# Placing the loads of ready weight blocks and of weight conversions in a fused attention, expert and gated-layer kernel

## The chip, the cores and the metric

The kernel runs on one NeuronCore of a Trainium2 chip. The metric is the device time of one execution in microseconds, taken as the median of several runs. The profile is of one execution; all other views come from its trace.

## The reference

The reference is three layers in float32, one after the other. The first is masked attention over four batches of 576 positions and eight heads of 64. The second is a mixture of eight experts over N = 2304 tokens of width 512, in which a Sinkhorn iteration makes the weights P and every token goes through every expert:

```python
for e in range(E):                       # E = 8, w1[e]: 512 x 1024, w2[e]: 1024 x 512
    h = np.maximum(x @ w1[e], 0.0)
    out += P[:, e:e + 1] * (h @ w2[e])
```

The third is a gated layer with 1536 hidden columns:

```python
xn = x / np.sqrt(np.mean(x * x, axis=-1, keepdims=True) + 1e-6) * rms_g
g = xn @ w_gate
silu = g * (1.0 / (1.0 + np.exp(-g)))
return (silu * (xn @ w_val) @ w_out).astype(np.float32)
```

The three weights of the gated layer arrive as float64.

## The kernel before, in words

**Numbers.** Each float32 operand is split into a high and a low part, and a product is made of three matmuls: high by high, high by low, low by high. Large products are cut into two-by-two blocks and done with seven block products in place of eight (`PROD`, L944), so an operand is needed as seven block combinations, each with a high and a low part. A weight region has 14 places of 256 columns: seven high, seven low.

**Stages.** Attention and the first expert come first, up to about 330 us. Then 42 groups `n` follow (L1978), each an expert `g` from 1 to 7, a half of its hidden columns and a third `qd` of the tokens. A group has 14 steps: two regions `j` (rounds r = 0 and 1) of seven products. A step issues one up product (`product`, L1219: six matmuls of 384 columns), its evictions (`outcome_1`, L1358), a tick, one down unit of the group before (`unit`, L1812) and another tick. Group 41 is the last; then come 12 units that are left over (`PRE_UNITS`, L2061), and then the gated layer, in nine passes (L2129): three slices `p` of hidden columns, three token thirds each. A pass has two rounds of 14 steps; step 0 to 6 of a round use one region, step 7 to 13 the next. The pass works with regions 0 to 3 for its slice, so the first round uses regions 0 and 1 and the second round 2 and 3.

**Order of work.** Every engine runs its own program in order. The order is set when the program is written, by a counter `bg.now` that `bg.pump` raises by one: a pump is one *slot*, 28 to a group. `bg.later(1, f)` writes `f` at the next pump. A `Queue` (L81) holds steps with lags in slots: a step is written once its lag has passed since the step before it, at most one slot being made up for a late one. Of the queues, `prep` makes or loads first-layer weights, `prep2` second-layer weights, `norm` the normalised inputs of the gated layer, and `conv` the conversions below. `prep` and `conv` are made with `yields`: once `bg.tight` is set (from expert 7 on, L1981), they write nothing while a model of VectorE's backlog is above a limit; `prep` does so only up to eight items. `drain` writes out what is left under a tag.

**Conversions.** `convert` (L820) turns half a 128-row block of a float64 weight into float32 on VectorE: `load` brings 256 KB into `raw`, `head` (L837, L838), `number` (L844, L848), `tail` (L854, L855) and `whole` (L861) are seven instructions of 256 columns, and `store` writes 128 KB to a table in DRAM (`m2d`). `raw`, the work area `a` and the result `t` are single places in the tile `cv`; `raw` is read last by `tail`, `t` by the store. `conversion` (L869) gives the lags. At group 2 the queue `conv` receives 24 items, then eight combinations (`first_combos`, L885), then 16 items (L2000 to L2006). It stands still in every group whose number divides by three (`conv.paused`, L1999), and at group 39 what is left is written at once (L2011 to L2013). The last 32 items are queued at the second pass (L2142).

`first_combos` loads float32 blocks, makes their seven combinations (L900 is the first instruction, in `sums_1`), splits them and stores them to the table `w1d`: the *ready* weights of the gated layer's first slice, regions 0 to 3.

**Ready weights.** `ready_combos` (L935) loads a part of region 0 or 1 (up to 512 KB, L940) into `w1t`, into places that the last group's products have read. `prepare_1` (L1054) calls it for the parts of `PARTS_AT` after products 1, 3, 5 and 6 of group 41 and puts each into `prep`; `prep.drain(("w1", E, 1))` (L2072) writes out what `prep` still holds after the 12 left units. Right behind it, L2073 to L2079 load regions 2 and 3 in six transfers, 3584 KB in all, into `last_r`, a free x place, and three pieces of `w2t`.

**Normalised inputs.** `norm_blocks` (L1479) makes, per third of the tokens, three times four parts: `plain` and `keep` (stores at L1499), then `add1`, `add2`, four `part` steps (ScalarE and VectorE at L1489 and L1490) and `keep2` (five stores at L1523). The next block's `part` steps write over tiles that `keep2` reads. Their results in `xnd` are loaded as x blocks (`load_block`, L1154), the first ones before the first pass.

All DMAs named here are issued by SyncE (SP), one after the other; an issue waits on SP for what it depends on. The evictions that free the two up-product buffers `ub` are, in the groups, copies on ScalarE and the additions of `with_more` (L1254) on VectorE, and in the passes also the multiplies at L1411 and L1425.

Of the kernel before, what the change touches and what calls it, by code (L numbers as in the profile page):

```python
# [10 lines left out]
U32 = mybir.dt.uint32  # L11
# [103 lines left out]
def kernel(  # L115
# [17 lines left out]
    E, _, F = w1.shape  # L133
# [27 lines left out]
    EARLY = 2  # L161
    EARLY_AT = (5, 6)
    SUMS = 24
    CONV_WAIT = (6, 4)
    PRE_WAIT = 6
    PRE_UNITS = 12
    LAG = 12
    TURN_AT = (29, 30, 31, 32, 33, 34), (32, 33, 34, 35, 36, 37)
# [2 lines left out]
    Y0_AT = (7, 10, 13, 16, 19)  # L171
    READ = 7
    LAST_READ = 16
    STEP = 1.5
    PACE = 1.2
    PARTS_AT = {0: 0, 1: 1, 3: 2, 5: 3, 6: 4}
# [640 lines left out]
        return us  # L817


    def convert(nm, f, half):  # L820

        n = KC * P // 2
        raw = cv[:, : 2 * n].bitcast(U32)
        pair = raw.rearrange("p (n t) -> p n t", t=2)
        a, t = cv[:, 2 * n : 3 * n].bitcast(U32), cv[:, 3 * n : 4 * n]

        def load():
            if nm == "o":
                nc.sync.dma_start(out=raw, in_=m2_out[f * P : (f + 1) * P, half * 2 * n : (half + 1) * 2 * n])
            else:  # L830
                src = (m2_gate if nm == "g" else m2_val)[half * n : (half + 1) * n, f * 2 * P : (f + 1) * 2 * P]
                nc.sync.dma_start(
                    out=raw.rearrange("p (c n) -> p c n", c=KC // 2), in_=src.rearrange("(c p) n -> p c n", p=P)
                )

        def head():
            nc.vector.tensor_scalar(out=a, in0=pair[:, :, 1], scalar1=0x7FFFFFFF, scalar2=None, op0=ALU.bitwise_and)  # L837
            nc.vector.tensor_scalar(  # L838
                out=t, in0=a.bitcast(F32), scalar1=LOW_HEAD, scalar2=HIGH_HEAD, op0=ALU.max, op1=ALU.min
            )  # L840
            return n

        def number():
            nc.vector.tensor_scalar(  # L844
                out=a, in0=t.bitcast(U32), scalar1=3, scalar2=0x3FFFFFFF,
                op0=ALU.logical_shift_left, op1=ALU.bitwise_and,
            )
            nc.vector.scalar_tensor_tensor(  # L848
                out=a, in0=pair[:, :, 1], scalar=0xC0000000, in1=a, op0=ALU.bitwise_and, op1=ALU.bitwise_or
            )  # L850
            return 2 * n

        def tail():
            nc.vector.tensor_scalar(out=t.bitcast(U32), in0=a, scalar1=0xFF800000, scalar2=None, op0=ALU.bitwise_and)  # L854
            nc.vector.scalar_tensor_tensor(  # L855
                out=t, in0=pair[:, :, 0], scalar=2.0**-52, in1=t, op0=ALU.mult, op1=ALU.mult
            )
            return 2 * n

        def whole():  # L860
            nc.vector.tensor_tensor(out=t, in0=a.bitcast(F32), in1=t, op=ALU.add)  # L861
            return n

        def store():
            nc.sync.dma_start(out=m2d[nm][:, f, half * n : (half + 1) * n], in_=t)

        return load, head, number, tail, whole, store

    def conversion(items, wait, quick=False):  # L869

        for n, (nm, f, half) in enumerate(items):
            load, head, number, tail, whole, store = convert(nm, f, half)
            tag = nm, f
            if n == 0:
                conv.add([(WRITE, load)], tag)
            step = 1 if quick else STEP
            conv.add([(wait, head), (step, number), (step, tail)], tag)
            if n + 1 < len(items):
                conv.add([(step, whole), (0 if quick else 1, convert(*items[n + 1])[0])], tag)
                conv.add([(0 if quick else 2, store)], tag)  # L880
            else:
                conv.add([(step, whole), (WRITE, store)], tag)


    def first_combos(s, c):  # L885

# [25 lines left out]
        def high(src):  # L912
            nc.scalar.activation(h[:, : src.shape[1]].bitcast(F32R), src, AF.Copy)
# [7 lines left out]
        def store(src, spots):  # L921
# [4 lines left out]
                        in_=t[:, P * at : P * (at + n)].rearrange("p (k n) -> p k n", k=n),  # L926
                    )

        return load, [
            (PRE_WAIT, sums_1), (STEP, sums_2), (STEP, lambda: high(raw)), (STEP, lambda: low(raw)),  # L930
            (1, lambda: store(raw, ((0, 0, 2), (2, 5, 1), (3, 2, 1)))), (5, lambda: high(both)), (STEP, lambda: low(both)),
            (1, lambda: store(both, ((0, 3, 2), (2, 6, 1)))),
        ]

    def ready_combos(j, part):  # L935

# [117 lines left out]
    def prepare_1(g, j, part=None):  # L1054

        if part is None:
            for part in range(5):
                prepare_1(g, j, part)
            return
        if g == E:  # L1060
            prep.add([(PACE, lambda: ready_combos(j, part))], ("w1", g, j))
        else:
            if part == 0:
                stages[g, j] = combine(region(g, j), raw_1)
            prep.add(stages[g, j][part], ("w1", g, j))
        n = (g, j + 1) if j < 3 else (g + 1, 0)
        if part == 4 and n[0] < E + NPASS and n[0] != E:
            prep.add([(WRITE, lambda: load_1(*n))])
# [463 lines left out]
    with tc.manual_schedule():  # L1532
# [445 lines left out]
        for n, (g, hh, qd) in enumerate(groups):  # L1978
# [20 lines left out]
            conv.paused = n % NQD == 0 and n < NGP - 3  # L1999
            if n == 2:  # L2000
                conversion(conv_items[:24], CONV_WAIT[0])
                for s in range(4):
                    for c in range(2):
                        load, steps = first_combos(s, c)
                        conv.add([(WRITE, load)] + steps, "combos")
                conversion(conv_items[24:40], CONV_WAIT[0])  # L2006
            if ends and n < NGP - 1:
                g2, hh2, _ = groups[n + 1]
# [60 lines left out]
            (w2t[:, 0:3].rearrange("p f s n -> p (f s n)"), (0, 1, 2, 3, 4, 5, 6, 7, 8, 9, 10, 11)),  # L2069
            (xt_flat[:, 7680:8192], (12, 13)),  # L2070
        ])
        prep.drain(("w1", E, 1))  # L2072
        for j, parts in (  # L2073
            (2, ((last_r[:, :1792], 0), (x_slot(gone_x)[:, :1280], 7), (last_r[:, 1792:], 12), (x_slot(gone_x)[:, 1280:], 13))),
            (3, ((w2t[:, 0:3].rearrange("p f s n -> p (f s n)"), 0), (xt_flat[:, 7680:8192], 12))),
        ):
            ready = w1d[:, j].rearrange("p i k c m -> p (i k c m)")
            for t, at in parts:
                nc.sync.dma_start(out=t.bitcast(F32), in_=ready[:, 256 * at : 256 * at + t.shape[1]])  # L2079
        prep.add([(WRITE, lambda: load_1(E + 1, 0))])  # L2080

        def downs(r):
# [46 lines left out]
        for n, (p, qd) in enumerate(passes):  # L2129
# [9 lines left out]
            bg.drain("x")  # L2139
            if n == 1:  # L2140
                conv.yields = False
                conversion(conv_items[40:], CONV_WAIT[1], True)  # L2142
            for j in range(NG // 2):
                gs, hs = {}, {}
                first_round = (n, j) == (0, 0)
# [8 lines left out]
                for ci, s in enumerate((2 * j, 2 * j + 1)):  # L2154
# [8 lines left out]
                    for i, (wk, xk, which, begins) in enumerate(PROD):  # L2163
# [8 lines left out]
                        step = 7 * ci + i  # L2172
                        if first_round:
                            tick()
                            if PRE_UNITS + step < LAG:
                                second(14 * NGP + PRE_UNITS + step)
                            if step in LAST_TURN:
                                t = LAST_TURN.index(step)
                                if t == 0:
                                    spares[NGP - 1] = spare_of(NGP - 1)  # L2180
                                turn_tile(groups[-1][2], t, db[t % 3], spares[NGP - 1])
                        else:
                            bg.pump()
# [54 lines left out]
```

## Time and profile before

| | |
|---|---|
| median of 3 runs | 2094.93 us |
| lowest and highest run | 2087.04 and 2097.82 us |
| profiled execution | 2093.68 us, of which the span of the trace is 2091.9 |
| busy, matmuls on TensorE (PE) | 2009.6 us in 13611 instructions |
| busy, VectorE (DVE) | 1591.9 us |
| busy, ScalarE (ACT) | 1305.5 us |
| busy, GpSimd (POOL) | 268.1 us |
| moved by DMA | 434.24 MB, mean 208 GB/s |

PE is busy nearly throughout, so the engine views that matter are those of its gaps. A wait row names the engine and line that stood, what released it, the total, the count and the longest. A timeline row gives the start, the duration, the instruction and, in brackets, the idle time before it with its releaser; instructions of one kind in a row are merged. SPq is the queue of SP; a merged SPq row spans from the first issue to the end of the last, waits included. The clock is the granted share of 2.4 GHz.

### The profile page before, as it was taken

How to read it: one execution, taken by the hardware profiler on the slowest of the kernel's cores; microseconds unless marked ns; L12 is line 12 of the kernel's file. 1: busy time of each engine (PE TensorE's matmuls, PEld its weight loads, DVE VectorE, ACT ScalarE, POOL GpSimd, SP SyncE). 2: the span in 40 equal slices, each digit the busy share in tenths (PEclk: the TensorE clock that was granted, in tenths of full speed). 3: DMA queues.
4: the chain of work that ended last, by engine and by line, in shares of the span. 5: the costliest groups of instructions: out<-in, count | busy, mean ns of one | idle time of the engine just before them, and what ended most of it. 6: DMA issues, size and time to landing. Idle time of an engine off the chain costs nothing. (4 is left out here: it accounts for less than half of the span.)

```text
span 2091.9 us, 37504 instructions
## 1 busy us (share of the span) xinstructions
PE 2009.6 (96%) x13611; PEld 1920.0 (92%) x13611; DVE 1591.9 (76%) x3387; ACT 1305.5 (62%) x2932; POOL 268.1 (13%) x304
## 2 busy tenths in 40 slices
PE   8999999999999999999999999999998689999999
PEld 7888888999999999999999999999997578888998
DVE  3777747979786887968787798888888677887644
ACT  6766325777776877768787777777765433423332
POOL 6443200010211111111011101110100000000000
PEclk9999999999999999999999999999999999999999
DMA  6687576677988989796888978888666875354341
GB/s 182 174 241 212 171 262 203 216 256 190 270 208 223 245 222 278 194 277 190 240 230 226 260 196 239 216 217 234 157 214 218 270 226 177 118 176 139 112 166 61
DMA packets 356297, 434.24 MB, mean 208 GB/s; under 512 B 81296, under 2 KB 258384, under 8 KB 355984
## 3 DMA queue, kind: packets, MB, share of 16 engines
q1 hardware_dynamic: 317344, 363.48, 53.6%
q0 software_dynamic: 38768, 68.36, 18.6%
q8 instruction: 107, 1.75, 0.3%
q14 instruction: 78, 0.64, 0.1%
HBM read 301.75 MB, written 130.02 MB: 206 GB/s over the span
## 5 line engine op out<-in xcount | busy, mean ns | idle before, releaser
L1222 PE MATMUL ub<-xt,w1t 128*128 128x384 f32 x2328 | 471.5, 339 | 34.3 <-DVE fa L1254 17.8
L1222 PEld LDWEIGHTS ub<-xt,w1t 128*128 128x128 f32 x2328 | 396.5, 190 | 43.3 <-DVE fa L1254 21.6
L1222 PE MATMUL ub<-xx,w1t 128*128 128x384 f32 x1956 | 394.4, 338 | 10.2 <-DVE fa L1254 5.2
L1822 PE MATMUL db<-w2t,ht 128*128 128x256 f32 x2772 | 382.2, 282 | 3.0 <-DVE ht L1250 1.6
L1822 PEld LDWEIGHTS db<-w2t,ht 128*128 128x128 f32 x2772 | 369.5, 190 | 3.8 <-DVE ht L1250 1.9
L1822 PE MATMUL db<-w2t,hx 128*128 128x256 f32 x2520 | 347.2, 282 | 3.4 <-ACT hx L1247 2.0
L1222 PEld LDWEIGHTS ub<-xx,w1t 128*128 128x128 f32 x1956 | 331.0, 189 | 19.6 <-DVE fa L1254 8.4
L1822 PEld LDWEIGHTS db<-w2t,hx 128*128 128x128 f32 x2520 | 334.4, 189 | 4.8 <-ACT hx L1247 2.5
L1254 DVE TENSOR_TENSOR fa<-ub,fa 128x384 f32<-128x384 f32 x360 | 199.2, 554 | 129.9 <-PE ub L1222 122.4
L1373 ACT ACTIVATE fa<-fa 128x384 f32<-128x384 f32 x252 | 132.3, 525 | 193.5 <-DVE fa L1254 192.9
L1886 POOL DMA_DIRECT2D y1d<-acc x99 | 113.9, 1150 | 840.8 <-ACT acc L1879 376.8
L1250 DVE TENSOR_TENSOR ht<-fa,ht 128x384 fp32r<-128x384 f32 x344 | 189.6, 552 | 29.3 <-ACT ht L1247 28.7
L1879 ACT ACTIVATE acc<-acc,prob 128x256 f32<-128x256 f32 (+1 forms) x351 | 190.7, 572 | 15.2 <-DVE acc L1854 14.3
L1247 ACT ACTIVATE ht<-fa 128x384 fp32r<-128x384 f32 x344 | 177.3, 518 | 32.8 <-DVE fa L1425 32.3
L1250 DVE TENSOR_TENSOR hx<-fa,hx 128x384 fp32r<-128x384 f32 x316 | 174.6, 552 | 29.0 <-ACT hx L1247 27.8
L1247 ACT ACTIVATE hx<-fa 128x384 fp32r<-128x384 f32 x316 | 162.2, 519 | 48.0 <-DVE fa L1425 44.5
L1328 DVE TENSOR_TENSOR fa<-fa 128x384 f32<-128x384 f32 x336 | 185.7, 553 | 5.0
L1365 ACT COPY fa<-ub 128x384 f32<-128x384 f32 x252 | 119.4, 474 | 84.7 <-PE ub L1222 83.5
L1854 DVE TENSOR_TENSOR acc<-db,acc 128x768 f32<-128x768 f32 (+1 forms) x117 | 143.0, 1222 | 31.8 <-PE db L1822 31.1
L1843 ACT COPY acc<-db 128x768 f32<-128x768 f32 x156 | 124.3, 797 | 14.6 <-PE db L1822 10.4
L1390 ACT COPY fa<-ub 128x384 f32<-128x384 f32 x108 | 51.5, 477 | 86.6 <-PE ub L1222 86.5
L982 DVE TENSOR_TENSOR w1t<-fa,w1t 128x256 fp32r<-128x256 f32 (+1 forms) x160 | 83.7, 526 | 9.2 <-ACT w1t L979 9.0
(261 smaller groups left out, 3062.9 us busy)
## 6 DMA issues: line engine op xcount, KB each, us to landing
xt<-xdt SPq DMA_DIRECT2D x111, 768.0 KB
xx<-xdt SPq DMA_DIRECT2D x92, 768.0 KB
y1d<-acc POOLq DMA_DIRECT2D x72, 384.0 KB, 7.4
y1d<-acc POOLq DMA_DIRECT2D x36, 768.0 KB, 9.2
xt<-xnd SPq DMA_DIRECT2D x25, 768.0 KB
xx<-xnd SPq DMA_DIRECT2D x24, 768.0 KB
fa<-in_moe_w_dram SPq DMA_DIRECT2D x56, 256.0 KB
raw<-in_moe_w_dram SPq DMA_DIRECT2D x52, 256.0 KB
```

Source lines behind the costliest of these rows:

```text
L1222: nc.tensor.matmul(ps[:, :TH], w[i][:, c], x[:, k, c], start=first and c == 0 and n == 0, stop=c == 1 and n == 2, skip_group_check=True,)
L1247: nc.scalar.activation(h[0], src, func)
L1250: engine.tensor_tensor(out=h[1], in0=src, in1=h[0].bitcast(F32), op=ALU.subtract)
L1254: nc.vector.tensor_tensor(out=out, in0=ps, in1=more, op=ALU.add)
L1328: nc.vector.tensor_tensor(**kw)
L1365: nc.scalar.copy(z[nm], ps)
L1373: nc.scalar.activation(z[nm], z[nm], AF.Relu)
L1822: nc.tensor.matmul(spot(k, m), hm[x], w[y], start=BEGIN[k] and r == 0 and m != 1 and i == 0, stop=r == 1 and i == 2, skip_group_check=True,)
L1843: nc.scalar.copy(a, ps)
L1854: nc.vector.tensor_tensor(out=a, in0=ps, in1=a, op=ALU.add)
L1879: nc.scalar.activation(a, a, AF.Copy, scale=prob[:, tile_of(qd, b), g : g + 1])
L1886: nc.gpsimd.dma_start(out=y, in_=t, accum_op=ALU.add)
```

## The change

Six places change. The waits of `conv` are new (`CONV_WAIT`, `PRE_WAIT`). `convert` takes a place for `raw` and uses two places for `t` in turn. In `conversion` the load of the next item follows `tail`, half a slot later, in place of `whole`; the store follows `whole` by three slots. `first_combos` loads the next combination's blocks before its own last store. The last 32 conversions go through `late_conversion`, with two places for `raw`, loads two items ahead and the second place in a part of `fa`. `ready_combos` is written at the next pump and no longer goes through `prep`; regions 2 and 3 are loaded by `load_last` at steps 4 and 11 of the first round of the gated layer.

```diff
--- before.py
+++ after.py
@@ -161,8 +161,8 @@
     EARLY = 2
     EARLY_AT = (5, 6)
     SUMS = 24
-    CONV_WAIT = (6, 4)
-    PRE_WAIT = 6
+    CONV_WAIT = (6.5, 2.5)
+    PRE_WAIT = 9
     PRE_UNITS = 12
     LAG = 12
     TURN_AT = (29, 30, 31, 32, 33, 34), (32, 33, 34, 35, 36, 37)
@@ -171,6 +171,7 @@
     Y0_AT = (7, 10, 13, 16, 19)
     READ = 7
     LAST_READ = 16
+    LOAD_LAST = (4, 11)
     STEP = 1.5
     PACE = 1.2
     PARTS_AT = {0: 0, 1: 1, 3: 2, 5: 3, 6: 4}
@@ -817,12 +818,16 @@
         return us
 
 
-    def convert(nm, f, half):
+    turns_c = [0]
+
+    def convert(nm, f, half, raw=None):
 
         n = KC * P // 2
-        raw = cv[:, : 2 * n].bitcast(U32)
+        raw = (cv[:, : 2 * n] if raw is None else raw).bitcast(U32)
         pair = raw.rearrange("p (n t) -> p n t", t=2)
-        a, t = cv[:, 2 * n : 3 * n].bitcast(U32), cv[:, 3 * n : 4 * n]
+        turns_c[0] += 1
+        i = 3 + turns_c[0] % 2
+        a, t = cv[:, 2 * n : 3 * n].bitcast(U32), cv[:, i * n : (i + 1) * n]
 
         def load():
             if nm == "o":
@@ -866,21 +871,27 @@
 
         return load, head, number, tail, whole, store
 
-    def conversion(items, wait, quick=False):
-
-        for n, (nm, f, half) in enumerate(items):
-            load, head, number, tail, whole, store = convert(nm, f, half)
-            tag = nm, f
-            if n == 0:
-                conv.add([(WRITE, load)], tag)
-            step = 1 if quick else STEP
-            conv.add([(wait, head), (step, number), (step, tail)], tag)
-            if n + 1 < len(items):
-                conv.add([(step, whole), (0 if quick else 1, convert(*items[n + 1])[0])], tag)
-                conv.add([(0 if quick else 2, store)], tag)
-            else:
-                conv.add([(step, whole), (WRITE, store)], tag)
-
+    def conversion(items, wait):
+
+        made = [convert(*x) for x in items]
+        conv.add([(WRITE, made[0][0])], items[0][:2])
+        for n, (_, head, number, tail, whole, store) in enumerate(made):
+            tag = items[n][:2]
+            conv.add([(wait, head), (STEP, number), (STEP, tail)], tag)
+            if n + 1 < len(made):
+                conv.add([(0.5, made[n + 1][0])], tag)
+            conv.add([(1, whole), (WRITE, store)], tag)
+
+    def late_conversion(items, wait):
+
+        made = [convert(*x, (None, fa[:, 4608:5120])[n % 2]) for n, x in enumerate(items)]
+        conv.add([(WRITE, made[0][0]), (0, made[1][0]), (WRITE, lambda: None)], items[0][:2])
+        for n, (_, head, number, tail, whole, store) in enumerate(made):
+            tag = items[n][:2]
+            conv.add([(wait, head), (STEP, number), (STEP, tail)], tag)
+            if n + 2 < len(made):
+                conv.add([(0, made[n + 2][0])], tag)
+            conv.add([(STEP, whole), (0, store)], tag)
 
     def first_combos(s, c):
 
@@ -926,11 +937,14 @@
                         in_=t[:, P * at : P * (at + n)].rearrange("p (k n) -> p k n", k=n),
                     )
 
-        return load, [
-            (PRE_WAIT, sums_1), (STEP, sums_2), (STEP, lambda: high(raw)), (STEP, lambda: low(raw)),
-            (1, lambda: store(raw, ((0, 0, 2), (2, 5, 1), (3, 2, 1)))), (5, lambda: high(both)), (STEP, lambda: low(both)),
-            (1, lambda: store(both, ((0, 3, 2), (2, 6, 1)))),
-        ]
+        def steps(then):
+            return [
+                (PRE_WAIT, sums_1), (STEP, sums_2), (STEP, lambda: high(raw)), (STEP, lambda: low(raw)),
+                (1, lambda: store(raw, ((0, 0, 2), (2, 5, 1), (3, 2, 1)))), (5, lambda: high(both)), (STEP, lambda: low(both)),
+                (0, then), (1, lambda: store(both, ((0, 3, 2), (2, 6, 1)))),
+            ]
+
+        return load, steps
 
     def ready_combos(j, part):
 
@@ -1058,7 +1072,7 @@
                 prepare_1(g, j, part)
             return
         if g == E:
-            prep.add([(PACE, lambda: ready_combos(j, part))], ("w1", g, j))
+            bg.later(1, lambda: ready_combos(j, part))
         else:
             if part == 0:
                 stages[g, j] = combine(region(g, j), raw_1)
@@ -1999,10 +2013,10 @@
             conv.paused = n % NQD == 0 and n < NGP - 3
             if n == 2:
                 conversion(conv_items[:24], CONV_WAIT[0])
-                for s in range(4):
-                    for c in range(2):
-                        load, steps = first_combos(s, c)
-                        conv.add([(WRITE, load)] + steps, "combos")
+                made_c = [first_combos(s, c) for s in range(4) for c in range(2)]
+                conv.add([(WRITE, made_c[0][0])], "combos")
+                for i, (_, steps) in enumerate(made_c):
+                    conv.add(steps(made_c[i + 1][0] if i + 1 < len(made_c) else lambda: None), "combos")
                 conversion(conv_items[24:40], CONV_WAIT[0])
             if ends and n < NGP - 1:
                 g2, hh2, _ = groups[n + 1]
@@ -2069,14 +2083,16 @@
             (w2t[:, 0:3].rearrange("p f s n -> p (f s n)"), (0, 1, 2, 3, 4, 5, 6, 7, 8, 9, 10, 11)),
             (xt_flat[:, 7680:8192], (12, 13)),
         ])
-        prep.drain(("w1", E, 1))
-        for j, parts in (
-            (2, ((last_r[:, :1792], 0), (x_slot(gone_x)[:, :1280], 7), (last_r[:, 1792:], 12), (x_slot(gone_x)[:, 1280:], 13))),
-            (3, ((w2t[:, 0:3].rearrange("p f s n -> p (f s n)"), 0), (xt_flat[:, 7680:8192], 12))),
-        ):
+        last_parts = (
+            ((last_r[:, :1792], 0), (x_slot(gone_x)[:, :1280], 7), (last_r[:, 1792:], 12), (x_slot(gone_x)[:, 1280:], 13)),
+            ((w2t[:, 0:3].rearrange("p f s n -> p (f s n)"), 0), (xt_flat[:, 7680:8192], 12)),
+        )
+
+        def load_last(j):
             ready = w1d[:, j].rearrange("p i k c m -> p (i k c m)")
-            for t, at in parts:
+            for t, at in last_parts[j - 2]:
                 nc.sync.dma_start(out=t.bitcast(F32), in_=ready[:, 256 * at : 256 * at + t.shape[1]])
+
         prep.add([(WRITE, lambda: load_1(E + 1, 0))])
 
         def downs(r):
@@ -2139,7 +2155,7 @@
             bg.drain("x")
             if n == 1:
                 conv.yields = False
-                conversion(conv_items[40:], CONV_WAIT[1], True)
+                late_conversion(conv_items[40:], CONV_WAIT[1])
             for j in range(NG // 2):
                 gs, hs = {}, {}
                 first_round = (n, j) == (0, 0)
@@ -2172,6 +2188,8 @@
                         step = 7 * ci + i
                         if first_round:
                             tick()
+                            if step in LOAD_LAST:
+                                load_last(2 + LOAD_LAST.index(step))
                             if PRE_UNITS + step < LAG:
                                 second(14 * NGP + PRE_UNITS + step)
                             if step in LAST_TURN:
```

## Rows read from the trace of the kernel before

**Rows 1.** Page, busy shares; then what PE waited for (total us, times, longest).

```profile
PE 2009.6 (96%) x13611; PEld 1920.0 (92%) x13611; DVE 1591.9 (76%) x3387; ACT 1305.5 (62%) x2932; POOL 268.1 (13%) x304
...
PE ub L1222 <- DVE fa L1411: 15.3, 6, 11.4
```

**Rows 2.** Stretches: us; busy PE, PEld, DVE, ACT, POOL; clock, DMA share, GB/s.

```profile
943.00:950.00 7.00, 6.82 (x37) 6.82 (x38) 5.91 (x15) 5.84 (x14) 0.00 (x0) 0.77 0.23 64
...
1621.60:1657.50 35.90, 20.23 (x110) 18.34 (x108) 21.42 (x49) 18.08 (x43) 1.70 (x2) 0.86 0.96 330
...
1634.60:1646.00 11.40, 0.06 (x1) 0.00 (x0) 1.37 (x4) 1.81 (x5) 0.00 (x0) 0.70 1.04 376
...
1646.00:1657.50 11.50, 10.43 (x56) 9.77 (x56) 10.19 (x21) 6.41 (x14) 0.00 (x0) 0.85 0.76 218
```

**Rows 3.** Timelines of SP, ACT and PE: start, us, what, [idle before <-releaser].

```profile
1561.46 6.48 SPq L940 DMA_DIRECT2D w1t<-w1d  x2
...
1621.94 3.93 SPq L940 DMA_DIRECT2D w1t<-w1d  x6
...
1626.15 0.33 SPq L2079 DMA_DIRECT2D last_r<-w1d  x1
...
1633.16 7.17 SPq L1523 DMA_DIRECT2D xnd<-acc  x3
...
1644.18 0.42 ACT L1489 ACTIVATE acc<-acc 128x256 fp32r<-128x256 f32 x1 [10.78 <-DMA xnd<-acc]
...
1646.05 2.29 PE L1222 MATMUL ub<-xt,w1t 128*128 128x384 f32 x6 [11.39 <-DVE fa L1411]
```

**Rows 4.** Waits of PE and DVE, 360 to 1500, then 1699 to 1935; SP's, span.

```profile
PE ub L1222 <- DVE fa L1254: 13.0, 10, 5.0
...
DVE cv L838 <- DMA m2g<-cv: 10.9, 4, 3.7
...
PE ub L1222 <- DVE fa L1254: 6.5, 7, 2.3
...
PE ub L1222 <- DVE fa L1411: 3.0, 4, 1.8
...
DVE cv L837 <- DMA cv<-in_moe_w_out_dram: 13.4, 11, 2.5
...
SPq L832 <- DVE cv L855: 217.6, 44, 13.2
```

**Rows 5.** Timelines of DVE and PE in the groups of the middle layers.

```profile
661.10 0.29 DVE L837 TENSOR_SCALAR cv<-cv 128x256 uint32<-128x256 uint32 x1 [3.09 <-DMA cv<-in_moe_w_gate_dram]
...
942.04 0.62 DVE L900 TENSOR_TENSOR cv<-cv 128x128 f32<-128x128 f32 x2 [8.32 <-DMA cv<-m2g]
...
943.18 2.29 PE L1222 MATMUL ub<-xt,w1t 128*128 128x384 f32 x6 [5.02 <-DVE fa L1254]
```

**Rows 6.** Timelines of DVE and SP: conversions, two of them the last before group 39.

```profile
438.25 0.28 DVE L837 TENSOR_SCALAR cv<-cv 128x256 uint32<-128x256 uint32 x1
...
452.53 0.29 DVE L837 TENSOR_SCALAR cv<-cv 128x256 uint32<-128x256 uint32 x1
...
1492.24 0.28 DVE L837 TENSOR_SCALAR cv<-cv 128x256 uint32<-128x256 uint32 x1
...
1498.64 0.34 SPq L865 DMA_DIRECT2D m2v<-cv  x1
...
1850.66 0.43 DVE L848 SCALAR_TENSOR_TENSOR cv<-cv 128x256 uint32<-128x256 uint32 x1
```

**Rows 7.** Timelines of SP and DVE: two late conversion loads and the heads behind.

```profile
1692.86 2.32 SPq L829 DMA_DIRECT2D cv<-in_moe_w_out_dram  x1
...
1700.86 0.30 DVE L837 TENSOR_SCALAR cv<-cv 128x256 uint32<-128x256 uint32 x1 [2.45 <-DMA cv<-in_moe_w_out_dram]
...
1703.29 0.34 SPq L829 DMA_DIRECT2D cv<-in_moe_w_out_dram  x1
...
1706.34 0.29 DVE L837 TENSOR_SCALAR cv<-cv 128x256 uint32<-128x256 uint32 x1 [0.52 <-DMA cv<-in_moe_w_out_dram]
```

## The prediction

> **What bounds the kernel now.** I read the page's busy shares first, then who PE waited for, then the timeline of each engine around every PE stall. PE is busy 96% of the span, so time can come only from its stalls and from matmuls on a lowered clock, some 82 us of idle at most. The releasers at the top of the list of waits are DVE's add L1254, which clears the two up-product buffers, and its multiply L1411, with one stall of 11.4 us [rows 1]. DVE works in order, so the question is what held DVE.
>
> The single large stall lies in the last layer's first round. PE stops near 1634.6 and resumes at 1646.05; ACT stood 10.78 us for a store `xnd<-acc`, and DVE for ACT [rows 3]. The store is keep2 of `norm_blocks`: the next block's `part` steps overwrite the tile it reads. SP was late with it: at 1621.94 it began six ready-weight loads (L940), at 1626.15 six more (L2079), and the store came at 1633.16 with waits between its pieces; only two L940 loads had gone out early, at 1561.46 [rows 3]. By the shapes in the code that is 2.6 MB (four of 512 KB, two of 256 KB) and 3.7 MB (3584 KB) ahead of a store on which two engines wait. The round ran at 330 GB/s [rows 2].
>
> The other stalls are small and of one kind. Between 360 and 1500 us PE lost 13.0 us in ten waits for L1254, and there DVE stood at the heads of conversions and combinations: for loads at L837 and L900, and for the store that still reads the one buffer t at L838 [rows 4]. One event shows the law: DVE idled 8.32 us before a combination, and PE then lost 5.02 [rows 5]. So PE tolerates about 3.3 us (8.32 - 5.02) of a held DVE, and the rest is lost. From 1699 to 1935 the same pattern gives 6.5 and 3.0 us of PE waits for DVE, with 13.4 us of DVE waits for the loads of `m2_out` alone [rows 4].
>
> **The change, part by part; the sum is against the profiled 2093.68 us, which is 1.25 below the median of the runs.**
>
> *Ready weights as places come free, regions 2 and 3 at steps 4 and 11.* The loads are the same fourteen. The six late L940 loads move from 1622 into the last group, 1572 to 1595, where each waits on SP for the product that reads its place; the norm stores queued behind them get there up to one step of 2.1 us later (two slots, below), and x loads follow only at 1606, so I cost the move at nothing; without that cover it would be the 2.1 us. The L2079 loads move behind the first keep2. It is then issued when its data is ready, near 1626, and lands before ACT wants the tile at 1633, so the 11.39 us go. What is late next is DVE: in the 11.5 us after the stall it was busy 10.19, PE on a clock of 0.85 [rows 2]; a faster PE clock there returns at most 11.5 - 10.19 = 1.3. Against that, the second keep2 now queues behind region 2's 1.83 MB, 5 us at 376 GB/s [rows 2]; its tile is wanted a block later, nine steps of the norm queue, each at least a slot, or 9.5 us. I take -11, between -13 (all of both) and -5 (those 5 us and 1 more reappear).
>
> Here a limit on transfers speaks against it. The round moved 330 GB/s x 35.9 us = 11.85 MB. Without the early 2.6 it must move 9.2 MB in 35.9 - 11.4 = 24.5 us, or 376 GB/s, just what the 11.4 us of the stall showed [rows 2]; region 3, 1.83 MB, is wanted only in the next round, which leaves 7.4 MB and 302 GB/s. By rows it fits. The Trainium skill ("DMA: Bandwidth & Descriptors", Specifications) puts the HBM limit of a core at about 358 GB/s; the 376 row, which counts both directions, lies above it, so the trace does not agree; by the rule an estimated 25.7 us for 9.2 MB would make this term -10.
>
> *Conversion loads sooner in the groups, t in two buffers.* A slot is (452.53 - 438.25) / 13.5 = 1.06 us [rows 6], 13.5 being the lags of one item: 6 + 3 x 1.5 + 1 + 2. A load was issued 2 + 6 = 8 slots before its head; now 1 + 3 + 6.5 = 10.5, so 2.6 us sooner. The longest L837 wait there was 3.09 [rows 5], so they all but go; L838 waits (10.9 us for one kind) go, since a store now has a whole item. A combination's load has 1 + 9 = 10 slots instead of 6, or 4.2 us: 8.32 becomes 4.1, of which PE sees 0.8. The prize is 13.0, and 7 x 0.23 = 1.6 of clock in the stretch after the 5.02 us stall, granted 0.77 (1.2 GHz for part of it) [rows 2]: 14.6. I leave 0.8 and about 2 for new collisions: -12, between -14.6 and -5.
>
> *The same queue gets longer.* An item now takes 6.5 + 3 + 0.5 + 1 + 3 = 14 slots; a combination stays at 22. I counted the queue by its lags, 28 slots a group, standing still in every third: the old one ends with one store left when group 39 empties it, and the trace agrees (last head 1492.24, last store 1498.64 [rows 6], and group 39 begins near 1499). The new one, 20 slots longer, is left with the rest of item 38 and all of 39 and 40. `while conv.items: conv.run()` then writes them into DVE's program at one place, and each load starts only after the previous item's tail. A load took 3.05 us from issue (1703.29) to its head (1706.34) [rows 7]. DVE is held for number and tail 1.43, load 3.05, head to tail 2.0, load 3.05, an item 2.42 (four instructions of 0.28 to 0.29, three of 0.42 to 0.43 [rows 6]): 11.95 us. Less 3.3 that is 8.6 of PE, and 1.6 of clock as in the 943 stretch: +10. Low end +3: loads that cost nothing leave 1.43 + 0.42 + 2 x 2.42 = 6.7 of work, less 3.3. High end +20: each load like the one of 1692.86, 8.0 us to its head at 1700.86 [rows 7], which is 2 x 4.95 more. By the fit that the Trainium skill gives on the same page ("DMA: Bandwidth & Descriptors", Anatomy of one DMA), 2.0 us plus bytes over 436 GB/s, a 256 KB load would take an estimated 2.6 us, and this term would be 0.9 smaller.
>
> *Two load buffers at the end.* Period 7 slots before and after. A load led its head by 4 slots; now by 1.5 + 7 + 2.5 = 11. The longest wait of its largest kind is 2.5 us [rows 4], and seven slots are over 6, so the waits go. The prize is 6.5 + 3.0 = 9.5 of PE; some of it follows other work of DVE. I take -6.5, between -9.5 and -2.
>
> **Sum:** -11 - 12 + 10 - 6.5 = -19.5, so 2093.7 - 19.5 = 2074. All best ends: -13 - 14.6 + 3 - 9.5 = -34 (2060); all worst: -5 - 5 + 20 - 2 = +8 (2102).
>
> **The rivals.**
> 1. *The emptied queue costs little* (+3 instead of +10) and no new collision comes (2 more): 2065. For it: L940's loads show that SP can run well ahead of DVE. Against: a load there still needs the tail before it, and DVE cannot pass a head that waits.
> 2. *The burst only moves.* Regions 2 and 3 hold up later norm stores, or PE at step 14 or 21, and the 11 us come back in the same two rounds, as under a lower transfer rate than the stall's. 2085. Against: region 2 and region 3 have ten steps each, 10 x 24.5 / 14 = 17 us, for 5 us of transfer.
> 3. *The emptied queue meets slow loads*, both of 8 us: +10, 2084.
> 4. *SP blocks: slower.* SP is in order. A conversion load stood 2.5 slots behind the tail that frees its buffer, now 0.5, so SP waits there up to 2.1 us longer, with x-block loads behind it. It waited there 217.6 us in 44 waits already [rows 4]. It decides from the point where a block has less than 2.1 us to spare. If 20 of 40 group items hit: 20 x 2.1 = +42, 2116. Against: a place is reloaded nine steps, some 19 us, before its use, and no list of PE's waits there names an x load.
>
> That the change does not do what it says can be left aside for the loads, which are written out by hand; whether the waits it aims at are gone is rivals 2 and 3.
>
> **How the numbers follow.** Forecast 0.55, rival 1 0.15, rival 2 0.15, rival 3 0.07, rival 4 0.08. About 0.5% (10.5 us, below 2084.5 or above 2105.4) can be told from no change. Faster: forecast and rival 1, 0.70. Same: rivals 2 and 3, 0.22. Slower: rival 4, 0.08. The range runs from 2060, all best ends, to 2089, beyond rivals 2 and 3; it leaves out rival 4 and a tenth more.
>
> **What would show it.** Right: no PE stall near 11 us in the first round; L940 spread over 1561 to 1595; keep2 issued within 2 us of its data; no L838 waits; PE waits for L1254 in the groups down to a few us, but one stall of 7 to 10 us just after group 39 begins, with two L832 loads 5 us apart; almost no L837 waits at the end. Wrong: PE waiting for `last_r`, `w2t` or an x block, SP's x loads slipping, or a DVE wait for `xnd<-acc` above 5 us.

## The result and the profile after

The changed kernel takes 2069.75 us (median of 4 runs, 2067.86 to 2073.57) against 2095.21 before: a ratio of 0.9887, with a 95% interval of 0.9856 to 0.9919. That is faster by 25.5 us, or 1.1%. The profiled execution of the changed kernel took 2073.57 us, the highest of the four; the stages below are of that execution.

First the page of the changed kernel, busy time, share of the span and instructions of each engine:

```profile
PE 2006.9 (97%) x13611; PEld 1922.7 (93%) x13611; DVE 1591.7 (77%) x3387; ACT 1305.7 (63%) x2932; POOL 268.6 (13%) x304
```

The matmuls and the vector work are the same [rows 1]; only the time between them is less. Cutting both spans at the same PE instructions shows where. The cuts are the first column sum of the groups (338.75 before, 343.24 after), the first product of the gated layer (1621.61, 1621.36), the first product with `last_r` (1657.61, 1645.49) and the first product of the second pass (1685.49, 1673.56).

| stage, us | before | after | difference |
|---|---|---|---|
| up to the groups | 338.75 | 343.24 | +4.5 |
| 42 groups and left units | 1282.86 | 1278.12 | -4.7 |
| first round | 36.00 | 24.13 | -11.9 |
| second round | 27.88 | 28.07 | +0.2 |
| from the second pass on | 406.41 | 397.94 | -8.5 |

The first stage holds nothing of the change. It lay between 336.7 and 343.2 us in the profiles of this case. The group stage lay between 1278.7 and 1282.9 with the code of before (the kernel before and two runs below) and between 1277.5 and 1278.1 with the changed code (the changed kernel and three runs below), so a difference of one stage between two profiles is good to some 4 us, and the -4.7 starts from the longest of three. The other stages add to -24.9, close to the 25.5 between the medians.

**The first round.** The timelines of SP and PE of the changed kernel, with the loads L954 and L2094 (L940 and L2079 of [rows 3]), the first and second keep2 (L1537) and the product that stood 11.39 us:

```profile
1561.69 6.49 SPq L954 DMA_DIRECT2D w1t<-w1d  x2
...
1598.14 0.68 SPq L954 DMA_DIRECT2D w1t<-w1d  x1
...
1611.59 1.19 SPq L954 DMA_DIRECT2D w1t<-w1d  x1
...
1624.20 2.54 SPq L1537 DMA_DIRECT2D xnd<-acc  x3
...
1630.49 0.89 SPq L2094 DMA_DIRECT2D last_r<-w1d  x1
...
1634.99 5.35 SPq L1537 DMA_DIRECT2D xnd<-acc  x5
...
1640.38 0.47 SPq L2094 DMA_DIRECT2D w2t<-w1d  x1
...
1635.21 1.32 PE L1236 MATMUL ub<-xt,w1t 128*128 128x384 f32 x6 [0.48 <-DVE fa L1425]
```

keep2 leaves SP at 1624.20 and not at 1633.16, and the product waits 0.48 us. In the kernel before, SP itself had been held on its way to keep2: its waits from 1616 to 1634 us show the L2079 loads, and then keep2 (L1523), standing until ready-weight loads issued earlier had landed:

```profile
SPq L2079 <- DMA w1t<-w1d: 3.5, 4, 1.1
...
SPq L1523 <- DMA w1t<-w1d: 1.3, 2, 1.0
```

So the bytes ahead of keep2 delayed it even before it was issued. The stretch view gives the changed round with a us behind it, in the columns of [rows 2], and below it stands PE's largest wait from 1621.36 to 1645.40:

```profile
1621.60:1646.50 24.90, 19.69 (x114) 17.65 (x112) 21.92 (x50) 17.89 (x43) 1.70 (x2) 1.00 1.09 364
...
PE ub L1236 <- ACT fa L1404: 3.0, 2, 2.2
```

DVE is now the busiest engine, 21.92 of 24.9 us, and PE's clock is full. Of PE's remaining waits 3.0 us are for a copy of ACT and only 0.5 for each of two lines of DVE, so that DVE alone bounds the round is not shown. The bytes fitted: 364 GB/s, where 376 was worked out. So the limit weighed in the prediction did not bind: this too lies above 358 GB/s. The Trainium skill itself says elsewhere ("HBM Reference", Specifications (TRN2)) that 358 is a core's share when both cores of a pair stream, and that one streaming alone measures about 425; this kernel runs on one core, and its rows, 364 and 376, lie between the two and agree.

**The groups.** The waits of PE from 360 to 1486 us, all behind DVE, then the timelines of DVE, SP and PE around 1490:

```profile
PE ub L1236 <- DVE fa L1268: 1.2, 5, 0.2
PE db L1836 <- DVE hx L1264: 0.2, 1, 0.2
```

```profile
1485.81 0.29 DVE L842 TENSOR_SCALAR cv<-cv 128x256 uint32<-128x256 uint32 x1
...
1488.03 0.37 SPq L837 DMA_DIRECT2D cv<-in_moe_w_val_dram  x1
...
1491.92 0.29 DVE L842 TENSOR_SCALAR cv<-cv 128x256 uint32<-128x256 uint32 x1 [3.46 <-DMA cv<-in_moe_w_val_dram]
...
1494.14 0.37 SPq L837 DMA_DIRECT2D cv<-in_moe_w_val_dram  x1
...
1497.18 0.29 DVE L842 TENSOR_SCALAR cv<-cv 128x256 uint32<-128x256 uint32 x1 [2.61 <-DMA cv<-in_moe_w_val_dram]
...
1499.42 0.42 DVE L866 TENSOR_TENSOR cv<-cv 128x256 f32<-128x256 f32 x1
...
1502.97 2.29 PE L1236 MATMUL ub<-xt,w1t 128*128 128x384 f32 x6 [11.93 <-DVE fa L1268]
```

The 13.0 us of [rows 4] are 1.2. In their place stands one stall of 11.93 us. It lies just where group 39 empties the queue: three conversions behind one another on DVE, from 1485.81 to 1499.84. The second and third wait for loads that are issued only when the item before has let go of the buffer. The clock is lower behind the stall too, 0.65 in this stretch:

```profile
1500.00:1512.00 12.00, 9.03 (x46) 9.03 (x47) 10.80 (x20) 7.03 (x15) 1.29 (x1) 0.65 0.64 176
```

**The end.** The same 236 us behind the start of the second pass as in [rows 4], here 1687 to 1923, waits of PE and of DVE:

```profile
PE ub L1236 <- DVE fa L1268: 1.8, 3, 1.0
PE ub L1236 <- DVE fa L1439: 1.7, 3, 0.7
PE ub L1236 <- DVE fa L1425: 1.1, 1, 1.1
...
DVE cv L842 <- DMA cv<-in_moe_w_out_dram: 2.3, 1, 2.3
```

Of 13.4 us at the heads of the `m2_out` items 2.3 are left, and PE's waits for L1268 and L1425 fall from 6.5 + 3.0 to 1.8 + 1.1 us, so by 6.6. The stage is shorter by 8.5; these waits do not account for the other 2 us.

### The profile page after: what moved, and what is told of

Read it like the earlier page. It is cut to its first block, busy times and chain, and to the rows that moved or that the text cites. A ratio compares the mean times of both kernels' runs of the same rounds, so it can differ in the third digit from the quotient of the medians.

```text
span 2071.5 us, 37534 instructions
## 1 busy us (share of the span) xinstructions
PE 2006.9 (97%) x13611; PEld 1922.7 (93%) x13611; DVE 1591.7 (77%) x3387; ACT 1305.7 (63%) x2932; POOL 268.6 (13%) x304
## 5 line engine op out<-in xcount | busy, mean ns | idle before, releaser
L1268 DVE TENSOR_TENSOR fa<-ub,fa 128x384 f32<-128x384 f32 x360 | 199.8, 555 | 142.4 <-PE ub L1236 133.9
```

The costliest lines, as they stand in the source:

```text
L1268: nc.vector.tensor_tensor(out=out, in0=ps, in1=more, op=ALU.add)
```

## The experiments

Theory: each part acts in its own stage, and the queue that got longer puts a new stall before group 39. The rivals are with each run. Times are medians; ratios are to the kernel before in the same session, with 95% intervals. The changed kernel was timed in the first session alone, and the kernel before had medians of 2095.21, 2097.64, 2096.44 and 2096.58 us in the four, so a difference to the changed kernel is less sure than a ratio. Stages are cut as above.

### One part alone

Ready weights alone, on the kernel before:

```diff
-            prep.add([(PACE, lambda: ready_combos(j, part))], ("w1", g, j))
+            bg.later(1, lambda: ready_combos(j, part))
...
-        prep.drain(("w1", E, 1))
-        for j, parts in (
...
+                            if step in LOAD_LAST:
+                                load_last(2 + LOAD_LAST.index(step))
```

> The kernel before with the ready-weight part alone (parts of regions 0 and 1 written at the next pump, regions 2 and 3 at steps 4 and 11); conversions as before. My theory, each part acts in its own stage and they add: the first round of the gated layer shrinks from 36.0 to about 24 us, nothing else moves, so 11 to 12 us below before, about 2083. Rival, the burst only moves: the round shrinks but the next two rounds or the stores take it back, within 4 us of before.

2084.92 us, ratio 0.9929 (0.9909 to 0.9950). The first round took 25.51 us, the second 26.82, the rest 407.09. The burst did not come back in the rounds behind, so that rival falls.

The groups' conversions alone, with the old code for the last 32 and for the ready weights:

```diff
-    CONV_WAIT = (6, 4)
-    PRE_WAIT = 6
+    CONV_WAIT = (6.5, 2.5)
+    PRE_WAIT = 9
...
-                conversion(conv_items[40:], CONV_WAIT[1], True)
+                conversion_old(conv_items[40:], 4, True)
```

> The kernel before with the changed lags, the load behind tail and two places for t in the groups alone; ready weights and the last 32 conversions as before. My theory: PE loses about 2 us to L1254's waits in the groups instead of 13, but one stall of about 12 us stands just before group 39, so the stage from the first group to the first round takes 4 to 6 us less than the 1282.9 of before and the whole about 2090. Rival, the stall before group 39 comes from the ready-weight loads or another change: it is not here, and the whole is about 2079.

2092.88 us, ratio 0.9971 (0.9955 to 0.9988), as expected. The group stage took 1277.55 us, the first round 37.22. The timeline of PE shows both large stalls side by side:

```profile
1496.68 2.29 PE L1252 MATMUL ub<-xt,w1t 128*128 128x384 f32 x6 [11.90 <-DVE fa L1284]
...
1639.08 2.29 PE L1252 MATMUL ub<-xt,w1t 128*128 128x384 f32 x6 [11.78 <-DVE fa L1441]
```

The stall before group 39 belongs to the conversions, and the one in the first round does not.

Two load buffers for the last 32 alone:

```diff
-                conversion(conv_items[40:], CONV_WAIT[1], True)
+                late_conversion(conv_items[40:], 2.5)
```

> The kernel before with the two load buffers for the last 32 conversions alone. My theory: DVE's waits at the heads of these conversions fall from 20 us to about 3, and the time from the second round on falls by 6 to 8 us: about 2088. Rival, DVE would have been late there anyway (its own work, the stores of the normalised blocks): under 3 us, about 2093.

2083.41 us, ratio 0.9929 (0.9909 to 0.9949), so -14 us and more than expected. The profile is of the fastest of the six executions (2078.34). In it the time from the second pass on was 396.04 us, 10.4 less than before, which is this part; the group stage, whose program is the same, came out at 1278.66, 4.2 less, for a reason that is not shown. The rival (under 3 us) falls. The three parts alone give -12.7, -4.8 and -14.2 against 2097.64, in sum -31.7; together they gave -25.5. With intervals of 3 to 7 us on each of the four differences, an excess of 6 us is no evidence that the parts interact.

### The queue that is emptied at group 39

First the same queue with shorter items, so that by count it is empty in time:

```diff
-    CONV_WAIT = (6.5, 2.5)
+    CONV_WAIT = (6, 2.5)
```

> The changed kernel with the head's wait in the groups at 6 slots instead of 6.5, so that an item takes 13.5 slots again and by count the queue is empty in group 38. My theory: the stall of 11.9 us before group 39 is gone with its 1.6 us of lowered clock, at the price of at most 3 us of new collisions (the load leads its head by 10 slots, not 10.5): 11 to 14 us below the changed kernel, 2056 to 2059. Rival, the stall comes from what DVE has to do there in any case: it stays, 2068 to 2071.

2054.85 us, ratio 0.9792 (0.9773 to 0.9812): 14.9 below the median of the changed kernel (20 by the two ratios), and faster than both kernels. The group stage took 1265.56 us, 12.6 less than in the changed kernel. PE's waits there, 360 to 1486:

```profile
PE ub L1236 <- DVE fa L1268: 3.5, 5, 1.6
```

The stall is gone, at a price of 2.3 us of new waits, with the largest of 1.6. The same slots saved in another place, in the last 16 items alone:

```diff
-                conversion(conv_items[24:40], CONV_WAIT[0])
+                conversion(conv_items[24:40], 5)
```

> The changed kernel with the head's wait at 5 slots for the last 16 items of the groups alone (12.5 slots an item there); the first 24 items keep 14 slots. By count the queue is empty in group 38. My theory, the written-out items are the cause of the stall before group 39, wherever the missing slots are saved: the stall is gone as with 6 slots for all, and the whole is 2053 to 2058, the last items having at most a few us of load waits. Rival, in the run with 6 slots for all it was the changed phase of all items that helped: the stall or other waits of 8 us or more remain here, 2064 or more.

2055.74 us, ratio 0.9815 (0.9793 to 0.9837); group stage 1266.49, PE waits for L1268 1.3 us in six from 360 to 1486. The rival falls: it is not the phase of all items that matters. But the queue was not empty as counted. The timelines of DVE and PE show the last item as one block at the place of the emptying, from its first instruction to its last:

```profile
1481.65 0.28 DVE L842 TENSOR_SCALAR cv<-cv 128x256 uint32<-128x256 uint32 x1
...
1483.88 0.43 DVE L866 TENSOR_TENSOR cv<-cv 128x256 f32<-128x256 f32 x1
...
1487.44 1.31 PE L1236 MATMUL ub<-xt,w1t 128*128 128x384 f32 x6 [0.88 <-DVE fa L1268]
```

Its head waited for no load, and the 2.66 us of DVE cost PE 0.88. So what costs is above all the loads between items that are written out together. In the run with 6 slots for all no such block stands there. And the dose the other way, more left over:

```diff
-                conversion(conv_items[24:40], CONV_WAIT[0])
+                conversion(conv_items[24:40], 9)
```

> The changed kernel with the head's wait at 9 slots for the last 16 items of the groups: by count one item more is left when the queue is emptied at group 39. My theory, the stall is the time DVE is held by the items written out there: one load of about 3 us and one item of 2.4 us more, so the stall grows from 11.9 to about 17.5 us and the whole to about 2075. Rival, the stall is a fixed cost of that place (the loads of the group's x blocks behind it): it stays near 12, 2070.

2077.51 us, ratio 0.9904 (0.9887 to 0.9922). Timelines of DVE and PE:

```profile
1485.58 0.29 DVE L842 TENSOR_SCALAR cv<-cv 128x256 uint32<-128x256 uint32 x1 [1.97 <-DMA cv<-in_moe_w_gate_dram]
...
1490.95 0.29 DVE L842 TENSOR_SCALAR cv<-cv 128x256 uint32<-128x256 uint32 x1 [2.71 <-DMA cv<-in_moe_w_gate_dram]
...
1496.22 0.29 DVE L842 TENSOR_SCALAR cv<-cv 128x256 uint32<-128x256 uint32 x1 [2.61 <-DMA cv<-in_moe_w_val_dram]
...
1501.58 0.29 DVE L842 TENSOR_SCALAR cv<-cv 128x256 uint32<-128x256 uint32 x1 [2.71 <-DMA cv<-in_moe_w_val_dram]
...
1507.37 2.29 PE L1236 MATMUL ub<-xt,w1t 128*128 128x384 f32 x6 [19.93 <-DVE fa L1268]
```

Four heads behind one another and a stall of 19.93 us: 0, 0.9, 11.9 and 19.9 us for none, one, three and four items. The fixed cost falls as a rival. The last step is 8.0, more than the 5.5 expected. DVE was held 20.6 us (from 1483.61 to 1504.24) against 14.0, which is 6.6: one more interval between heads, 5.4, and 1.97 for the first item's load, less 0.7 that the second load was faster. The other 1.4 is slack, the part of a hold that PE does not feel: the stall was 2.1 us shorter than the hold in the changed kernel and 0.7 here.

### Which edit to the conversions

The changed kernel with one place for `t` in the groups:

```diff
+        raw0 = raw
...
-        i = 3 + turns_c[0] % 2
+        i = 3 if raw0 is None and turns_c[0] <= 40 else 3 + turns_c[0] % 2
```

> The changed kernel with one place for t in the 40 conversions of the groups (loads and lags as changed). My theory, DVE waits again for the store that reads t at the second instruction of a head, some 10 to 17 us in all as before, of which PE sees 3 to 6: about 2074. Rival, the sooner load alone carries the gain, since the store has 6.5 slots instead of 6: within 1 us of the changed kernel.

2086.47 us, ratio 0.9954 (0.9939 to 0.9969): 16.7 lost to the changed kernel's median (14 by the two ratios), where about 4 were expected. DVE, waits for stores, 360 to 1500:

```profile
DVE cv L845 <- DMA m2g<-cv: 11.2, 2, 5.8
DVE cv L845 <- DMA m2v<-cv: 9.1, 2, 5.4
DVE cv L845 <- DMA m2o<-cv: 5.9, 1, 5.9
```

Five long waits, at 481, 575, 669, 763 and 858 us, about 94 us apart, which is some three groups, the period of the queue's pauses. One of these stores left SP at 562.71, behind x-block loads and four loads of second-layer weights, and DVE was let go at 574.55. With 14 slots, two items to a group, the same store can meet the same loads each time; that items of 13.5 slots drift past them is inferred from the irregular times of these waits in the kernel before. The rival falls. PE's waits in that window are 15.8 us, 14.4 more than in the changed kernel, while the group stage grew by 20.9; some of the other 6.5 us is clock (0.93 of full speed from 664 to 690 and from 857 to 880), the rest stays open.

And two places alone, on the kernel before:

```diff
-        a, t = cv[:, 2 * n : 3 * n].bitcast(U32), cv[:, 3 * n : 4 * n]
+        turns_c[0] += 1
+        i = 3 + (turns_c[0] // 2 % 2 if turns_c[0] <= 78 else 0)
+        a, t = cv[:, 2 * n : 3 * n].bitcast(U32), cv[:, i * n : (i + 1) * n]
```

> The kernel before with two places for t in turn in the 40 conversions of the groups; loads and lags as before. My theory, the two edits to the conversions act on different waits: those at the second instruction of a head (17 us of DVE in the groups) go, those at its first and at the combinations (21 us) stay; the large stall of 5.02 us stays and PE keeps 8 to 10 of its 14 us of waits: 4 to 6 us below before, about 2091. Rival, with loads as late as before the second place does nothing, since DVE then only waits sooner, at the first instruction: within 2 us of before.

2086.59 us, ratio 0.9953 (0.9935 to 0.9971). That is -10.0 (some -6 to -14 by the interval), about twice what was expected. The group stage took 1273.54 us, 9.3 less than before, or 5.1 less than the shortest such stage with the code of before. Waits of PE and DVE, 360 to 1486:

```profile
PE ub L1226 <- DVE fa L1258: 6.2, 5, 4.9
...
DVE cv L904 <- DMA cv<-m2g: 8.2, 1, 8.2
DVE cv L841 <- DMA cv<-in_moe_w_out_dram: 3.1, 1, 3.1
DVE cv L841 <- DMA cv<-in_moe_w_gate_dram: 3.0, 1, 3.0
```

No wait for a store is left, and the waits for loads stand as they were. So the edits act on different waits, as the theory has it, but with the store's waits gone the loads' waits of 2.4 to 3.1 us stand alone, and slack covers all but 0.65 us of each. What PE had paid for was mostly their meeting in one item. In the kernel before, the item whose head waited 3.09 us at 661.10 [rows 5] waited again for the store:

```profile
665.14 0.30 DVE L838 TENSOR_SCALAR cv<-cv 128x256 f32<-128x256 f32 x1 [3.74 <-DMA m2g<-cv]
...
665.96 2.01 PE L1222 MATMUL ub<-xt,w1t 128*128 128x384 f32 x6 [3.50 <-DVE fa L1254]
```

The two waits, 6.83 us, less the slack of 3.3 that the prediction read off are the 3.5 that PE lost. Two more such items cost 1.31 and 0.83; the three make 5.6 of the 6.8 us by which PE's waits for this line fell.

### Which loads the first round waited for

The changed kernel with regions 2 and 3 back ahead of the round:

```diff
+        load_last(2)
+        load_last(3)
...
-                            if step in LOAD_LAST:
-                                load_last(2 + LOAD_LAST.index(step))
```

> The changed kernel with the six loads of regions 2 and 3 (3.67 MB) back at their place ahead of the first round; parts of regions 0 and 1 stay early. My theory, the first round waits for the bytes queued ahead of keep2's stores: of the 6.3 MB of before 2.6 are gone, 7 us at 376 GB/s, so a stall of 4 to 5 us stands in the round, which takes 28 to 29 us instead of 24.1; whole about 2074. Rival, the early parts of regions 0 and 1 alone make the gain (region 1 is what step 7 needs): the round stays at 24, 2070.

2075.97 us, ratio 0.9898 (0.9881 to 0.9914). The round took 33.25 us, 4 to 5 more than expected. The stall is 6.43 us where 4 to 5 were expected, and the granted clock of the round is 0.85 where the changed kernel has 1.00, which the expectation had left out. Timelines of SP, ACT and PE:

```profile
1624.11 6.08 SPq L1537 DMA_DIRECT2D xnd<-acc  x3
...
1635.28 0.42 ACT L1503 ACTIVATE acc<-acc 128x256 fp32r<-128x256 f32 x1 [5.82 <-DMA xnd<-acc]
...
1637.15 2.29 PE L1236 MATMUL ub<-xt,w1t 128*128 128x384 f32 x6 [6.43 <-DVE fa L1425]
```

The changed kernel with the parts of regions 0 and 1 late, as before:

```diff
-            bg.later(1, lambda: ready_combos(j, part))
+            prep.add([(PACE, lambda: ready_combos(j, part))], ("w1", g, j))
...
+        prep.drain(("w1", E, 1))
         last_parts = (
```

> The changed kernel with the parts of regions 0 and 1 back in their queue and written out behind the left units (2.6 MB ahead of keep2's stores); regions 2 and 3 stay at steps 4 and 11. My theory, bytes ahead of the stores: 1 to 2 us of stall in the round, 25 to 26 us instead of 24.1, whole about 2071. Rival, region 1 in time for step 7 is what matters: PE waits for these loads at step 7 and the round takes 29 us or more.

2071.64 us, ratio 0.9877 (0.9861 to 0.9893). The round took 26.88 us:

```profile
1630.03 0.42 ACT L1503 ACTIVATE acc<-acc 128x256 fp32r<-128x256 f32 x1 [1.60 <-DMA xnd<-acc]
...
1631.89 1.31 PE L1236 MATMUL ub<-xt,w1t 128*128 128x384 f32 x6 [2.21 <-DVE fa L1425]
```

So the wait grows with the bytes ahead of keep2, though not in proportion: 0, 2.6, 3.7 and 6.3 MB give 0.5, 2.2, 6.4 and 11.4 us of stall, and rounds of 24.1, 26.9, 33.3 and 36.0 us. Much of it arises before keep2 is issued, which happens 2.8, 4.8, 7.3 and 11.6 us behind the first product of the round; SP's time for issuing the loads and its waits for bytes to land are not told apart by these runs. Most of the gain is in moving regions 2 and 3 (with them alone the round is 26.9, with the early parts alone 33.3); no run had PE wait for region 1's own data, so that rival falls.

## Why the prediction was right, point by point

**The ready weights: -11 forecast, -11.9 measured** (-10.5 alone). The chain was as told: bytes ahead of keep2, its tile wanted by ACT, DVE behind ACT, PE behind DVE. The two partial returns show it by dose. That DVE is the next bound is half right: it is the busiest engine, but PE's largest remaining wait is for ACT (3.0 us). One detail was off: a part of the early loads left SP only at 1598.14 and one at 1611.59, behind norm stores and x loads, and not all by 1595; no product waited for them.

**The groups without the stall before group 39: -12 forecast, -12 to -17 measured** (1265.56 and 1266.49 in the two runs without it, against 1278.66 to 1282.86 with the code of before). The mechanism held; by the kernel before's own profile the size was low, beyond the best end of -14.6. The term priced what DVE waited for one load or one store at a time; where both met in one item they had added up beyond the slack, and two places for `t` alone gave -9.3. Against that profile PE's waits fell by 9.5 to 11.7 us and the clock gave back up to 3 in the stretches behind the two large stalls; about 3 us are not accounted for.

**The emptied queue: +10 forecast, +12.6 measured** (1278.12 less 1265.56; +11.6 by 1266.49). Place, cause and form were as forecast, and the runs with none, one and four items in the block settle the cause. What was mis-sized is the stall, 11.93 us and not 8.6. DVE was held for 14.0 us and not 11.95: the head of item 38 also ran in the block (0.65), the first load took 3.89 us from issue to head and not 3.05 (0.84), and the items themselves took some 0.6 longer than summed. And the slack was 14.0 - 11.9 = 2.1 and not 3.3; that one event at 942 us gave a fixed slack was an assumption, and the runs show 0.7 to 3.3. The Trainium skill ("DMA: Bandwidth & Descriptors", Anatomy of one DMA) gives the fit, by which the prediction worked out an estimated 2.6 us for such a load, for DMAs that GpSimd issues. The loads here are issued by SP, and both took longer, 3.89 and 3.04 us.

**The last conversions: -6.5 forecast, -8.5 measured** (-10.4 alone). PE's waits for DVE fell by 6.6 us in the window of [rows 4], near the term; the rest of the gain is not accounted for.

**The rivals.** That the emptied queue costs little, and that it meets loads of 8 us: neither (3.9 and 3.0). That the burst only moves: shown wrong by the run with the ready weights alone. That SP blocks: SP waited longer at these loads, as worked out (217.6 us before), and no x load came late by more than 0.5 us. Waits of SP over the changed kernel's span, and PE's only wait for an x block:

```profile
SPq L837 <- DVE cv L860: 285.3, 46, 12.6
...
PE ub L1236 <- DMA xt<-xnd: 0.5, 1, 0.5
```

The sum was -19.5 to the profiled 2093.68. It came out at -25.5 between medians and at -20.1 between the profiled executions, of which the changed one lost 4.5 us in a stage that the change does not touch. By the stages three gains were larger than worked out, by up to 5, 2 and 1 us, and the loss by 2.6. That the errors partly cancel is luck, and so is the nearness of 2074 to the profiled 2073.57.

## What to carry to other kernels

In an in-order program a lag is also a budget: before lags are raised in a queue with a deadline, count its slots, since what is left at the deadline runs in one block with every load behind the first item exposed; then check the count in a trace, which here showed one item more than counted. Put bulk loads behind the small stores whose tiles are wanted next, since the store here came later the more bytes were issued ahead of it. Two short waits in one item add up before the slack is taken off (3.09 and 3.74 us cost 3.50 here), so remove the one that is cheaper to remove and look again.

## What the runs showed of the hardware that was not expected

SP's issue of a store can stand for bytes that were issued before it: in the kernel before, the L2079 loads and keep2 stood 4.8 us together on SP until earlier ready-weight loads had landed. In the run with one place for `t` and items of 14 slots, half of a group's 28, a store was late by 3.7 to 5.9 us every 94 us; with 13.5 slots, in the kernel before, such waits came at irregular times. Half a slot of lag for each item, 14 against 13.5, moved the time by 15 us in a kernel of 2070, by way of what was left in the queue at group 39.
